# Two attention chunks in plain float32, a pair of heads at a time, and the first halves of batches 0 and 1 ahead of the rest

## The chip, the cores and the metric

One core of one Trainium2 chip runs the whole program. The metric is the device time of one execution in microseconds (us), the median of repeated runs. A profile is one execution, taken by the hardware profiler; its engines are PE (TensorE, with PEld for its weight loads), DVE (VectorE), ACT (ScalarE), POOL (GpSimd) and SP (the queue that issues the DMAs).

## The reference

Windowed attention with a few sink columns, for 4 batches, 8 heads, 768 positions and 64 elements a head, and behind it a two-layer network with a squared ReLU:

```python
keep = is_sink | ((rel >= 0) & (rel < window))       # n_sink = 4, window = 128
scores = np.where(keep, (q @ k.T) / 8, -1e9)         # B, H, S, D = 4, 8, 768, 64
a = np.exp(scores - scores.max(-1)); a = a / (a.sum(-1) + 1e-9)
x = (a @ v)                                          # heads joined: 3072 x 512
out = (s * np.maximum(x @ w_in, 0) ** 2 + b) @ w_out # 512 -> 2048 -> 512
```

Inputs and outputs are float32; `w_in` and `w_out` lie in memory in a form from which the kernel has to make the two float32r parts (a high and a low one) of every weight.

## The kernel before

The 3072 positions are eight **chunks** of 384: two halves of each of the four batches, in the order batch 0 first half, batch 0 second half, batch 1 first half, and so on. For each chunk there is an attention part, which leaves the chunk's `x` as a high and a low float32r part, and a network part of 16 slices `f` of the hidden layer: `l1(f)` (12 products, L521), its squared ReLU (L524 to L529) and `l2(f)` (9 products, L540).

**The first phase** computes chunk 0's attention alone (`first_slots`, L412 on). It works head by head with plain float32 products: `fa` makes the scores of one block of 128 rows (L443; the queries of a head lie on one half of the partitions and the other half is zeroed, L426 and L427), masks them with a running minimum (DVE, L445) and takes exp with its sum (ACT, L449). `fn` forms 1/sum (L457, L458) and scales the rows by it on DVE (L460). `fb` transposes by TensorE (L468) and ACT copies the result out (L472). `fc` multiplies by the values (L480) and splits the result into `x` (L482 on ACT, L483 on DVE). A first half of a batch needs no keys of an earlier block, so its three row blocks see 128, 256 and 384 columns.

**The stages.** Behind that, stage `c` runs the network part of chunk `c` and, between its steps, the attention of chunk `c + 1` (`attn_slots`): the slots of the one are laid between the steps of the other. This attention uses float32r products in two parts. So queries, keys and values are split into a high and a low part (ACT L268, L271, L277; DVE L272; POOL L273, L278), the transposed scores too (ACT L321, DVE L322), sinks are handled apart (POOL L305 and the `psk`, `xsk` lines), and the division comes last (L378 to L384).

**The weights.** In the first phase and in stage 0 the weights are made too (`make_weight`): per slice, two ACT steps (L198, L199), two DVE steps (L200, L201), one POOL step (L203), one ACT step (L208) and a subtraction on DVE, for every fourth slice on POOL (L214). From stage 1 on they are ready.

Instructions go to each engine's queue in an order that a scheduler sets when the program is built; an engine takes its queue in that order. SP issues all DMAs: limits, queries, keys and values of chunk 0, then the scalars `s` and `b`, then weights. A DVE instruction at L682 scales `s`.

```python
for c in range(NC_):
    steps = moe_steps(k.x, store_at(c), wk, before if c == 0 else None, c == NC_ - 1)
    if c + 1 < NC_:
        k, slots = attn_slots(c + 1)
```

## Time and profile before

| | us |
|---|---|
| median of 3 runs (lowest, highest) | 783.11 (782.27, 783.18) |
| the profiled execution | 784.06 |
| its span in the profile | 782.2 |
| PE busy in the span | 736.0 (94%) |
| DVE, ACT, POOL busy | 510.5, 495.0, 263.4 |
| mean granted TensorE clock, share of full | 0.983 |

Busy time is the time in which an engine has an instruction under way. The share of the whole span mixes stages with different limits, so the stages have to be looked at one by one; the stores of each chunk's output mark where a stage ends.

### The profile page before, as it was taken

How to read it: one execution, taken by the hardware profiler on the slowest of the kernel's cores; microseconds unless marked ns; L12 is line 12 of the kernel's file. 1: busy time of each engine (PE TensorE's matmuls, PEld its weight loads, DVE VectorE, ACT ScalarE, POOL GpSimd, SP SyncE). 2: the span in 40 equal slices, each digit the busy share in tenths (PEclk: the TensorE clock that was granted, in tenths of full speed). 3: DMA queues.
4: the chain of work that ended last, by engine and by line, in shares of the span. 5: the costliest groups of instructions: out<-in, count | busy, mean ns of one | idle time of the engine just before them, and what ended most of it. 6: DMA issues, size and time to landing. Idle time of an engine off the chain costs nothing.

```text
span 782.2 us, 12150 instructions
## 1 busy us (share of the span) xinstructions
PE 736.0 (94%) x4036; PEld 656.5 (84%) x4036; DVE 510.5 (65%) x1251; ACT 495.0 (63%) x1231; POOL 263.4 (34%) x411
## 2 busy tenths in 40 slices
PE   6878887599999999999999999999999999999996
PEld 3656675489989999999989999999989999999985
DVE  5888899985676466665676466665676466653321
ACT  4896977766676576656676576656676576643222
POOL 3146567652333234232333234232333234210000
PEclk9998999989999999999999999999999999999999
DMA  7644304212111211112111211112111211001001
GB/s 275 268 148 176 111 14 160 85 34 75 43 44 53 85 47 52 49 43 76 43 43 53 86 47 53 49 43 76 43 43 53 85 47 53 28 1 41 1 1 44
DMA packets 28118, 54.21 MB, mean 69 GB/s; under 512 B 3600, under 2 KB 16528, under 8 KB 26128
## 3 DMA queue, kind: packets, MB, share of 16 engines
q1 hardware_dynamic: 28048, 53.36, 20.8%
q8 instruction: 34, 0.56, 0.3%
q14 instruction: 36, 0.29, 0.1%
HBM read 47.06 MB, written 6.29 MB: 68 GB/s over the span
## 4 chain that ended last, share of the span: by engine, by line
PE 77%; DVE 7%; ACT 6%; POOL 4%; issue 3%; DMA 1%; SPq 1%; POOLq 0%; DVEq 0%; ACTq 0%
PE h L521 31%; PE po L540 30%; PE o L354 5%; PE sc L294 2%; PE sc L293 2%; POOL w L203 2%; PE tp L317 2%; PE tp L316 2%; DVE w L201 1%; ACT w L199 1%; DVE wt L200 1%; PE o L480 1%; DMA sb<-in_s 1%; ACT sm L304 1%; ACT w L208 1%
## 5 line engine op out<-in xcount | busy, mean ns | idle before, releaser
L521 PE MATMUL h<-x,w 128*128 128x384 f32 x1536 | 301.1, 345 | 13.3 <-DVE r L526 7.2
L540 PE MATMUL po<-w,g 128*128 128x512 f32 x1152 | 298.5, 401 | 4.9 <-DVE g L529 3.7
L521 PEld LDWEIGHTS h<-x,w 128*128 128x128 f32 x1536 | 270.8, 191 | 21.4 <-issue 5.4
L540 PEld LDWEIGHTS po<-w,g 128*128 128x128 f32 x1152 | 209.4, 189 | 46.3 <-DVE g L529 5.5
L524 ACT ACTIVATE r<-h 128x384 f32<-128x384 f32 x128 | 62.8, 491 | 110.2 <-PE h L521 103.2
L298 DVE CUSTOM_DVE_ANT_0 sm<-sc,msk 128x272 f32<-128x272 f32 (+1 forms) x168 | 70.2, 418 | 82.4 <-PE sc L294 60.6
L529 DVE SCALAR_TENSOR_TENSOR g<-r,sb,g 128x384 fp32r<-128x384 f32 x128 | 87.2, 681 | 44.7 <-ACT g L528 42.6
L526 DVE SCALAR_TENSOR_TENSOR r<-h,sb,r 128x384 f32<-128x384 f32 x128 | 78.5, 613 | 52.7 <-ACT r L524 52.5
L305 POOL COPY psk<-sm 128x48 f32<-128x48 f32 x168 | 51.8, 309 | 168.4 <-ACT sm L304 167.3
L304 ACT ACTIVATE sm<-sm,negm 128x272 f32<-128x272 f32 (+1 forms) x168 | 85.3, 508 | 22.2 <-DVE negm L298 21.5
L528 ACT ACTIVATE g<-r,sb 128x384 fp32r<-128x384 f32 x128 | 78.8, 615 | 29.3 <-DVE r L526 29.0
L273 POOL TENSOR_TENSOR kl<-kraw,kh 128x544 fp32r<-128x544 f32 (+1 forms) x56 | 71.9, 1283 | 56.4 <-ACT kh L271 54.2
L321 ACT CAST hl<-tp 128x256 fp32r<-128x256 f32 (+1 forms) x168 | 59.1, 353 | 27.2 <-PE tp L317 26.6
L354 PE MATMUL o<-hl,vv 128*128 128x256 f32 (+1 forms) x400 | 71.6, 295 | 1.8 <-DVE hl L322 0.9
L322 DVE TENSOR_TENSOR hl<-tp,hl 128x256 fp32r<-128x256 f32 (+1 forms) x168 | 66.6, 398 | 8.0 <-ACT hl L321 6.1
L278 POOL TENSOR_TENSOR vv<-vraw,vv 128x256 fp32r<-128x256 f32 (+1 forms) x56 | 42.5, 758 | 60.7 <-ACT vv L277 58.7
L354 PEld LDWEIGHTS o<-hl,vv 128*128 128x128 f32 x400 | 55.0, 190 | 4.1 <-issue 1.4
L363 DVE TENSOR_TENSOR xm<-o,y 64x384 f32<-64x384 f32 x56 | 30.9, 552 | 31.5 <-ACT y L362 31.3
L294 PE MATMUL sc<-kl,qs 128*128 128x272 f32 (+1 forms) x168 | 48.7, 290 | 0.4 <-POOL kl L273 0.4
L293 PE MATMUL sc<-kh,qs 128*128 128x272 f32 (+1 forms) x168 | 47.9, 285 | 0.7 <-DVE qs L272 0.4
L272 DVE TENSOR_TENSOR qs<-qraw,qs 64x384 fp32r<-64x384 f32 x56 | 42.4, 758 | 6.2 <-ACT qs L268 4.5
L317 PE MATMUL tp<-identr,sm 128*128 128x128 f32 x168 | 46.0, 274 | 0.0
(113 smaller groups left out, 837.6 us busy)
## 6 DMA issues: line engine op xcount, KB each, us to landing
w<-in_w SPq DMA_DIRECT2D x15, 1024.0 KB, 10.0
kraw<-in_kT SPq DMA_DIRECT2D x32, 272.0 KB, 2.6
out<-ot SPq DMA_DIRECT2D x24, 256.0 KB, 2.0
qraw<-in_qT SPq DMA_DIRECT2D x28, 192.0 KB, 2.3
kraw<-in_kT SPq DMA_DIRECT2D x24, 208.0 KB, 2.4
vraw<-in_v SPq DMA_DIRECT2D x16, 256.0 KB, 2.6
vraw<-in_v SPq DMA_DIRECT2D x12, 192.0 KB, 2.3
vsraw<-in_vsk SPq DMA_DIRECT2D x28, 64.0 KB, 1.8
```

Source lines behind the costliest of these rows:

```text
L273: nc.gpsimd.tensor_tensor(out=hd.kl[:, :kw], in0=hd.k[:, :kw], in1=hd.kh[:, :kw].bitcast(F32), op=ALU.subtract)
L293: nc.tensor.matmul(sc[:, :n], hd.qs[:, qs], hd.kh[:, c0:c0 + n], start=True, stop=False)
L294: nc.tensor.matmul(sc[:, :n], hd.qs[:, qs], hd.kl[:, c0:c0 + n], start=False, stop=True)
L298: nc.vector.tensor_tensor_reduce(out=sm[:, :n], in0=sc[:, :n], in1=m, scale=-0.125, scalar=BIG, op0=ALU.add, op1=ALU.min, accum_out=negm[: ...
L304: nc.scalar.activation(sm[:, :n], sm[:, :n], AF.Exp, bias=negm[:, uu], scale=-1.0, accum_out=pp.zz[:, i, hh:hh + 1])
L322: nc.vector.tensor_tensor(out=lo, in0=tp[:, a:z], in1=hi.bitcast(F32), op=ALU.subtract)
L354: nc.tensor.matmul(hd.o[:, q0:q0 + n * P], hd.vv[:, kb, :], hd.hl[:, t, c0 * P:(c0 + n) * P], start=(hd.n == 0), stop=(i == BLK - 1 and kb ...
L521: nc.tensor.matmul(h[:, :CH], weight[f][:, 0, wi, cc * P:(cc + 1) * P], x[xi][:, cc, :], start=(i == 0), stop=(i == 11))
L526: nc.vector.scalar_tensor_tensor(out=r, in0=h[:, :CH], scalar=sw_ap, in1=r, op0=ALU.mult, op1=ALU.mult)
L528: nc.scalar.activation(gg[:, 0, :], r, AF.Identity, bias=b_ap, scale=1.0)
L529: nc.vector.scalar_tensor_tensor(out=gg[:, 1, :], in0=r, scalar=b_ap, in1=gg[:, 0, :].bitcast(F32), op0=ALU.add, op1=ALU.subtract)
L540: nc.tensor.matmul(po[tb], gg[:, gi, tsl], weight[f][:, 1, wi, :], start=(f == 0 and i == 0), stop=(f == NF - 1 and i == 2))
```

## The change

- The chunks are taken in another order: (0,0), (1,0), (0,1), (1,1), (2,0), (2,1), (3,0), (3,1) as (batch, half). Outputs go to the same places.
- Chunks 0 and 1, both first halves now, are computed by a new class `Plain` in float32 products. Stage 0 so lays plain attention between the network steps, and not the two-part kind.
- `Plain` works on a pair of heads. Its queries and keys lie as loaded: one head on partitions 0 to 63, the other on 64 to 127, and each score product reads one half. The value products write their 64 rows to one half of a bank's partitions, so that a pair shares one bank and one split into `x`.
- The scaling by 1/sum is on GpSimd, six instructions a pair. Of the copies out of the transposes (512 columns each), one in three is on ACT and two on DVE.
- `s` and `b` are loaded behind the first pair's queries and keys. Weight making in the first phase is one step ahead. `xm` has one buffer and not two; the masks stay for the whole program.

```diff
+ORDER = ((0, 0), (1, 0), (0, 1), (1, 1), (2, 0), (2, 1), (3, 0), (3, 1))
-E0, LB0, LC0 = 8, 4, 6
+E0 = 8
+FN, FB, FC = (4, 2), (6, 6), (9, 10)
-    m_all = first.tile([P, 6 * P], MDT, tag="m", name="m_all")
+    m_all = const.tile([P, 6 * P], MDT, tag="m", name="m_all")
-        k.c, k.b, k.half = c, c // 2, c % 2
+        k.c, (k.b, k.half) = c, ORDER[c]
-                pp.x = wk.tile([P, CH], F32, tag="xm", name="xm")
+                pp.x = wk.tile([P, CH], F32, tag="xm", name="xm", bufs=1)
-    def first_slots():
...
+    class Plain:
...
+            self.groups = ((0, 1, 2),) if c == 0 else ((0, 1), (2,))
...
+        def scores(self, pr, group):
...
+            for i in self.groups[group]:
+                for hh in range(2):
+                    hs = slice(hh * D, (hh + 1) * D)
+                    j = (i // 2, hh)
+                    if j not in banks:
+                        banks[j] = ps("sc")
+                    c0, n = (0, P, 0)[i], (i + 1) * P
+                    nc.tensor.matmul(banks[j][:, c0:c0 + n], pp.q[hs, i * P:(i + 1) * P], pp.k[hs, :n], start=True, stop=True)
...
+                    nc.vector.tensor_tensor_reduce(out=sm, in0=banks[(i // 2, hh)][:, c0:c0 + n], in1=m_full[i], scale=-0.125, scalar=BIG,
+                                                   op0=ALU.add, op1=ALU.min, accum_out=negm[:, uu])
+                    nc.scalar.activation(sm, sm, AF.Exp, bias=negm[:, uu], scale=-1.0, accum_out=pp.z[:, 0, i, hh:hh + 1])
+        def norm(self, pr):
+            pp = self.pairs[pr]
+            nc.vector.tensor_scalar(out=pp.z[:, 1], in0=pp.z[:, 0], scalar1=1e-9, scalar2=None, op0=ALU.add)
+            nc.vector.reciprocal(out=pp.z[:, 0], in_=pp.z[:, 1])
+            for i in range(BLK):
+                c0, n = (0, P, 0)[i], (i + 1) * P
+                for hh in range(2):
+                    sm = pp.sm[2 * (i // 2) + hh][:, c0:c0 + n]
+                    nc.gpsimd.tensor_scalar(out=sm, in0=sm, scalar1=pp.z[:, 0, i, hh:hh + 1], scalar2=None, op0=ALU.mult)
+        def turned(self, pr, part):
...
+            pos = (((0, 0), (2, 2)), ((1, 0), (1, 1)), ((2, 0), (2, 1)))[part]
+            for hh in range(2):
+                for j, (i, kb) in enumerate(pos):
+                    c0 = (0, P, 0)[i] + kb * P
+                    nc.tensor.transpose(tp[:, (2 * hh + j) * P:(2 * hh + j + 1) * P], pp.sm[2 * (i // 2) + hh][:, c0:c0 + P], ident)
...
+            cp = nc.scalar.copy if part == 0 else nc.vector.tensor_copy
+            cp(out, tp.rearrange("p (h k c) -> p h k c", h=2, c=P))
+        def values(self, pr):
...
+            for kb in range(BLK):
+                for hh in range(2):
+                    a = (0, 3, 5)[kb]
+                    hs = slice(hh * D, (hh + 1) * D)
+                    nc.tensor.matmul(o[hs, kb * P:CH], pp.v[:, kb, hh], pp.t[:, hh, a:a + BLK - kb].rearrange("p k c -> p (k c)"),
+                                     start=(kb == 0), stop=(kb == BLK - 1))
+            nc.scalar.copy(self.x[0][:, pr, :], o[:, :CH])
+            nc.vector.tensor_tensor(out=self.x[1][:, pr, :], in0=o[:, :CH], in1=self.x[0][:, pr, :].bitcast(F32), op=ALU.subtract)
...
-    k, slots = first_slots()
+    k, slots = plain_slots(0)
+    k.load_first(slice(0, 1))
+    nc.sync.dma_start(sb[:, 0:1], s.partition_broadcast(P))
+    nc.sync.dma_start(sb[:, 1:2], b.partition_broadcast(P))
+    constants()
+    k.load_first(slice(1, NCC))
+    k.load_values()
...
-        if i >= 22 and i % 2 == 0:
-            weights(NEARLY - 1, (i - 20) // 2)
+        if i >= 20 and i % 2 == 0:
+            weights(NEARLY - 1, (i - 18) // 2)
...
-            k, slots = attn_slots(c + 1)
+            k, slots = plain_slots(1) if c == 0 else attn_slots(c + 1)
```

The first place where rows move is SP's queue at the program's start. Before (`q_102`, `q_103`, `k_106`, `v_107` are chunk 0's queries of even and odd heads, keys and values, the first load of each the first pair's; `sb` holds `s` and `b`; `w_` are raw weights):

```order
L431 DMA q_102<-in_qT 64x384
L433 DMA k_106<-in_k 128x384
L431 DMA q_103<-in_qT 64x384
L434 DMA v_107<-in_v 128x384
L431 DMA q_102<-in_qT 64x3x384
L433 DMA k_106<-in_k 128x1152
L431 DMA q_103<-in_qT 64x3x384
L434 DMA v_107<-in_v 128x3x384
L493 DMA sb<-in_s 128x1
```

With the change:

```order
L431 DMA q_102<-in_qT 128x384
L432 DMA k_103<-in_k 128x384
L721 DMA sb<-in_s 128x1
L722 DMA sb<-in_b 128x1
L431 DMA q_102<-in_qT 128x3x384
L432 DMA k_103<-in_k 128x1152
```

The load of `s` moved from ninth to third place among these.

The second place is ACT's queue at the end of the first phase, up to the last pair's `x`. Before (`w4` to `w7` are tiles of raw weights, `x0_0` is the high part of chunk 0's `x`, `vs`, `qs`, `kh`, `vv` are chunk 1's split operands):

```order
L259 CAST vs_565<-vsraw_563 128x128
L268 CAST qs_568<-qraw_556 64x384
L271 CAST kh_570<-kraw_561 128x544
L482 CAST x0_0_104<-o0_498 64x384
L472 COPY tt0_490<-tp0_511 128x3x128
L277 CAST vv_575<-vraw_558 128x4x64
L198 ACTIVATE w4_263<-w4_263 128x1024
L199 ACTIVATE w4_263<-w4_263 128x1024
L482 CAST x0_0_104<-o0_518 64x384
```

With the change (`tf` is the copied transpose):

```order
L201 ACTIVATE w4_246<-w4_246 128x1024
L520 CAST x0_0_105<-o_403 128x384
L200 ACTIVATE w5_397<-w5_397 128x1024
L201 ACTIVATE w5_397<-w5_397 128x1024
L210 CAST w2_512<-w3_244 128x2x512
L200 ACTIVATE w6_399<-w6_399 128x1024
L509 COPY tf_414<-tp_415 128x2x2x128
L201 ACTIVATE w6_399<-w6_399 128x1024
L200 ACTIVATE w7_401<-w7_401 128x1024
L201 ACTIVATE w7_401<-w7_401 128x1024
L520 CAST x0_0_105<-o_442 128x384
```

The raw weights up to `w7` are now begun ahead of the last `x`, where before `w4` was the last. The whole queue up to that `x` holds 17 weight instructions with the change (seven each of L200 and L201, three of L210) and held 10 before (four of L198, four of L199, two of L208); the four casts for chunk 1 are gone.

The third place is POOL's queue in stage 0, with the change (`w6_399` and the like are raw weights, `smf` the exp'd scores of pair 0 of chunk 1, `zf` its 1/sum):

```order
L205 TENSOR_TENSOR w6_399<-w6_399 128x1024
L205 TENSOR_TENSOR w7_401<-w7_401 128x1024
L494 TENSOR_SCALAR smf_496<-smf_496,zf_489 128x128
L494 TENSOR_SCALAR smf_499<-smf_499,zf_489 128x128
L494 TENSOR_SCALAR smf_496<-smf_496,zf_489 128x256
L494 TENSOR_SCALAR smf_499<-smf_499,zf_489 128x256
L494 TENSOR_SCALAR smf_574<-smf_574,zf_489 128x384
L494 TENSOR_SCALAR smf_577<-smf_577,zf_489 128x384
L205 TENSOR_TENSOR w8_549<-w8_549 128x1024
```

The scalings of a pair stand as a block between weight steps, where before copies into `psk` and subtractions for keys, values and `x` stood.

## Rows read from the trace of the kernel before

**Rows 1.** The busy time of each engine by stage. The columns are: the stretch in us, its length, then busy us and instruction count of PE, PEld, DVE, ACT, POOL, the granted TensorE clock as a share of full, the DMA share and GB/s. The stretches are stage 0, stage 1 (beside the attention of a first half), stage 2 (beside that of a second half) and the last stage (no attention).

```profile
49.50:179.50 130.00, 104.86 (x517) 86.06 (x516) 117.02 (x196) 97.94 (x200) 82.37 (x74) 0.93 0.32 111
179.50:266.00 86.50, 86.01 (x494) 79.21 (x493) 55.39 (x148) 55.95 (x152) 28.12 (x52) 1.00 0.18 55
266.00:355.40 89.40, 89.08 (x518) 82.29 (x517) 57.64 (x148) 58.37 (x152) 29.38 (x52) 1.00 0.18 55
707.20:782.20 75.00, 68.47 (x342) 61.21 (x340) 19.94 (x33) 21.00 (x38) 1.01 (x1) 0.98 0.06 23
```

**Rows 2.** The timeline of the SP queue: the stores of a chunk's output, three at the end of each stage (start in us, length).

```profile
179.51 3.09 SPq L638 DMA_DIRECT2D out<-ot  x3
...
265.99 3.08 SPq L638 DMA_DIRECT2D out<-ot  x3
```

**Rows 3.** DVE in stage 0, by line and shape: output and inputs, count | busy us, mean ns | idle time before. These are lines of the two-part attention.

```profile
L272 DVE TENSOR_TENSOR qs<-qraw,qs 64x384 fp32r<-64x384 f32 x9 | 12.9, 1431 | 0.3
L298 DVE CUSTOM_DVE_ANT_0 sm<-sc,msk 128x272 f32<-128x272 f32 x24 | 10.4, 432 | 2.6 <-PE sc L294 2.3
...
L322 DVE TENSOR_TENSOR hl<-tp,hl 128x256 fp32r<-128x256 f32 x24 | 9.7, 414 | 0.1
...
L363 DVE TENSOR_TENSOR xm<-o,y 64x384 f32<-64x384 f32 x8 | 4.4, 549 | 0.1
...
L381 DVE TENSOR_TENSOR xm<-os,xm 128x384 f32<-128x384 f32 x4 | 2.2, 553 | 0.9 <-PE os L378 0.9
L382 DVE TENSOR_TENSOR xm<-zb,xm 128x384 f32<-128x384 f32 x4 | 2.2, 552 | 0.2
L370 DVE TENSOR_TENSOR xsk<-ts,xsk 32x384 fp32r<-32x384 f32 x4 | 2.2, 550 | 0.1
...
L298 DVE DVE_READ_ACCUMULATOR2_ANT negm<- 128x1 f32 x24 | 1.9, 80 | 0.0
```

**Rows 4.** DVE in the first phase, by line and shape, same columns.

```profile
L483 DVE TENSOR_TENSOR x<-o,x 64x384 fp32r<-64x384 f32 x8 | 4.4, 551 | 1.2 <-ACT x L482 0.9
L445 DVE CUSTOM_DVE_ANT_0 sm<-sc,m_all 128x384 f32<-128x384 f32 x8 | 4.4, 548 | 0.3 <-PE sc L443 0.2
L460 DVE TENSOR_SCALAR sm<-sm,z 128x128 f32<-128x128 f32 x8 | 4.2, 531 | 0.1
...
L445 DVE CUSTOM_DVE_ANT_0 sm<-sc,m_all 128x256 f32<-128x256 f32 x8 | 3.4, 420 | 1.3 <-PE sc L443 1.2
L460 DVE TENSOR_SCALAR sm<-sm,z 128x384 f32<-128x384 f32 x8 | 3.3, 411 | 0.0
L460 DVE TENSOR_SCALAR sm<-sm,z 128x256 f32<-128x256 f32 x8 | 2.8, 345 | 0.0
...
L445 DVE CUSTOM_DVE_ANT_0 sm<-sc,m_all 128x128 f32<-128x128 f32 x8 | 2.3, 284 | 1.7 <-PE sc L443 1.7
...
L445 DVE DVE_READ_ACCUMULATOR2_ANT negm<- 128x1 f32 x24 | 2.0, 81 | 0.0
L458 DVE RECIPROCAL z<-z 128x3 f32<-128x3 f32 x8 | 1.4, 174 | 0.2
...
L457 DVE TENSOR_SCALAR z<-z 128x3 f32<-128x3 f32 x8 | 1.3, 162 | 0.0
```

**Rows 5.** The timeline of TensorE in the first phase (start, length, instructions merged): six transposes, the value products of one head (six instructions, two for each of 384, 256 and 128 columns), and what starts behind them.

```profile
21.23 0.82 PE L468 MATMUL tp<-identr,sm 128*128 128x128 f32 x6
21.89 0.82 PE L443 MATMUL sc<-k,q 128*128 128x128 f32 x4
22.55 1.46 PE L480 MATMUL o<-tt,v 128*128 128x384 f32 x6
23.84 0.60 PE L468 MATMUL tp<-identr,sm 128*128 128x128 f32 x4
```

**Rows 6.** TensorE in the first phase, by line and shape: the longest form of the score products.

```profile
L443 PE MATMUL sc<-k,q 128*128 128x384 f32 x16 | 7.0, 520 | 0.0
```

**Rows 7.** The timeline of DVE: the instruction that scales `s`, with the idle time before it and what ended it.

```profile
13.34 0.15 DVE L682 TENSOR_SCALAR sb<-sb 128x1 f32<-128x1 f32 x1 [3.54 <-DMA sb<-in_s]
```

**Rows 8.** The timeline of ACT at the end of the first phase: a weight step, and the last high part of chunk 0's `x`.

```profile
49.36 1.13 ACT L199 ACTIVATE w<-w 128x1024 f32<-128x1024 f32 x1
50.51 0.48 ACT L482 CAST x<-o 64x384 fp32r<-64x384 f32 x1
```

**Rows 9.** ACT in the first phase, by line and shape.

```profile
L482 ACT CAST x<-o 64x384 fp32r<-64x384 f32 x8 | 3.8, 476 | 0.7 <-PE o L480 0.4
L472 ACT COPY tt<-tp 128x384 f32<-128x384 f32 x8 | 3.8, 475 | 0.1
...
L472 ACT COPY tt<-tp 128x256 f32<-128x256 f32 x8 | 2.9, 366 | 0.2 <-PE tp L468 0.2
...
L472 ACT COPY tt<-tp 128x128 f32<-128x128 f32 x8 | 2.1, 266 | 1.4 <-PE tp L468 1.3
```

**Rows 10.** POOL in stage 0, by line and shape: a subtraction with two inputs.

```profile
L384 POOL TENSOR_TENSOR x<-xm,x 128x384 fp32r<-128x384 f32 x3 | 4.3, 1421 | 2.6 <-ACT x L383 2.6
```

**Rows 11.** POOL in the first phase: a fill, which writes and reads nothing.

```profile
L140 POOL MEMSET psk<- 128x384 f32 x2 | 0.8, 418 | 0.1
```

**Rows 12.** The timeline of all engines in stage 2: the last reader of one pair's `xm`, and the first writer of the next pair's.

```profile
341.97 1.02 POOL L384 TENSOR_TENSOR x<-xm,x 128x384 fp32r<-128x384 f32 x1
...
344.62 0.54 DVE L363 TENSOR_TENSOR xm<-o,y 64x384 f32<-64x384 f32 x1
```

More of the change, by code (lines that the diff above doesn't have):

```diff
@@ new lines, in norm @@
+        def norm(self, pr):
+            pp = self.pairs[pr]
+            nc.vector.tensor_scalar(out=pp.z[:, 1], in0=pp.z[:, 0], scalar1=1e-9, scalar2=None, op0=ALU.add)
+            nc.vector.reciprocal(out=pp.z[:, 0], in_=pp.z[:, 1])
+            for i in range(BLK):
+                c0, n = (0, P, 0)[i], (i + 1) * P
+                for hh in range(2):
+                    sm = pp.sm[2 * (i // 2) + hh][:, c0:c0 + n]
+                    nc.gpsimd.tensor_scalar(out=sm, in0=sm, scalar1=pp.z[:, 0, i, hh:hh + 1], scalar2=None, op0=ALU.mult)
@@ new lines, in turned @@
+        def turned(self, pr, part):
+            pp = self.pairs[pr]
+            if part == 0:
+                pp.t = (wk if self.c else first).tile([P, 2, 2 * BLK, P], F32, tag="hl" if self.c else "tt0", name="tf", bufs=2)
+            tp = (ps if self.c else po_bank)("tp")
+            pos = (((0, 0), (2, 2)), ((1, 0), (1, 1)), ((2, 0), (2, 1)))[part]
[3 more added lines that the diff above has]
+                    nc.tensor.transpose(tp[:, (2 * hh + j) * P:(2 * hh + j + 1) * P], pp.sm[2 * (i // 2) + hh][:, c0:c0 + P], ident)
+            out = pp.t[:, :, part:part + (6 if part == 0 else 3):(5 if part == 0 else 2)]
+            cp = nc.scalar.copy if part == 0 else nc.vector.tensor_copy
+            cp(out, tp.rearrange("p (h k c) -> p h k c", h=2, c=P))
@@ new lines, in values @@
+        def values(self, pr):
+            pp = self.pairs.pop(pr)
+            o = ps("o")
+            for kb in range(BLK):
+                for hh in range(2):
[5 more added lines that the diff above has]
+            nc.vector.tensor_tensor(out=self.x[1][:, pr, :], in0=o[:, :CH], in1=self.x[0][:, pr, :].bitcast(F32), op=ALU.subtract)
@@ new lines, in po_bank, with plain_slots, at @@
+    def po_bank(name):
+        return psO.tile([P, 512], F32, tag="po", name=name)
+    def plain_slots(c):
+        k = Plain(c)
+        k.turn = 0
+        todo = {}
+        def at(t, fn, *a):
+            todo.setdefault(max(t, 0), []).append((fn, a))
+        first_one = c == 0
+        for pr in range(H // 2):
+            t = 6 * pr
+            at(t - (0 if first_one else 6), k.load, pr)
+            for g in range(len(k.groups)):
+                at(t + 2 * g, k.scores, pr, g)
+            for part in range(3):
+                at(t + FB[first_one] + part, k.turned, pr, part)
+            at(t + FN[first_one], k.norm, pr)
+            at(t + FC[first_one], k.values, pr)
@@ L488, in slot @@
         def slot(t):
             def f():
-                if t == 0:
-                    load()
-                    constants()
-                    nc.sync.dma_start(sb[:, 0:1], s.partition_broadcast(P))
-                    nc.sync.dma_start(sb[:, 1:2], b.partition_broadcast(P))
-                if t < n:
-                    fa(*units[t])
-                if t % BLK == BLK - 1 and t < n:
-                    for i in range(BLK):
-                        fn(t // BLK, i)
-                if 0 <= t - LB0 < n:
-                    fb(*units[t - LB0])
@@ L503, in f @@
-                if 0 <= t - LC0 < n and (t - LC0) % BLK == BLK - 1:
-                    fc((t - LC0) // BLK)
+                for fn, a in todo.get(t, ()):
+                    fn(*a)
             return f
-        return k, [slot(t) for t in range(n + LC0)]
+        return k, [slot(t) for t in range(max(todo) + 1)]
     def moe_steps(x, store, wk, before=None, last=False):
@@ L636, in f @@
         def f(tb, ot):
-            r0 = c * CH + tb * P
+            r0 = (2 * ORDER[c][0] + ORDER[c][1]) * CH + tb * P
             nc.sync.dma_start(out[r0:r0 + P, :], ot)
```

105 lines of the change are left out of this document (45 added, 60 removed).

## The prediction

> **What bounds the kernel now.** I read the busy times by stage first, since the share of the whole span hides that there are two kinds of stage. From stage 1 on TensorE is busy for 86.0 of 86.5 us or 89.1 of 89.4 us, at full clock, and DVE and ACT for only some 56 to 58 us [rows 1]: there only TensorE's work counts. Stage 0 is different: 130.0 us, with DVE busy for 117.0 (0.90), TensorE for 104.9 at a mean clock of 0.93, and POOL for 82.4 [rows 1]. Weight making and the two-part attention both sit on DVE there, and TensorE waits. The stage boundaries are the stores of a chunk's output [rows 2]. The last stage, which has no attention, takes 68.5 us of TensorE; so the attention beside stage 1 costs 17.5 us of it and the one beside stage 2 20.6 us. The first phase, up to 49.5 us, is a chain over all engines: nobody is full, and one stall stands in the DVE queue, 3.54 us in front of the scaling of `s`, because the load of `s` lands late [rows 7].
>
> The sums are made against the profiled execution, 784.06 us, which is 0.95 us above the median of the runs, 783.11.
>
> **Stages 1 to 7.** Stage 1 now runs beside the attention of (0,1), a second half, where it ran beside (1,0), a first half. The five stages behind it keep their kinds. So one stage of 86.5 us becomes one of 89.4 us: **+2.9 us**, certain as long as TensorE sets these stages. `xm` with one buffer adds a wait in the DVE queue: the next pair's first write (L363) behind POOL's last read (L384). At the closest pass that I found in stage 2, the read ends at 342.99 us and the write begins at 344.62 us [rows 12], so 1.6 us are left and I cost it at nothing. Without that cover, scores and splits queued behind L363 on DVE would wait, and TensorE for them.
>
> **Stage 0, DVE.** Out go the two-part lines: the `qs` splits (8 of the 9, 11.5 us), masks 10.4 and their accumulator reads 1.9, `hl` 9.7, and the four lines of `xm` and `xsk` 11.0; together 44.5 us [rows 3]. In come, for one plain chunk: masks 4.4 + 3.4 + 2.3 and accumulator reads 2.0, so 12.1 us; half of the 1/sum lines, 1.4 us, since a pair shares them; the splits of `x`, four of 384 columns on 128 partitions, half of 4.4 us, 2.2 [rows 4]. The copies of 512 columns on DVE have no row. Their bounds: 0.55 us, the two-input read of 384 columns, from below, and 0.73 us, the same stretched to 512 columns, from above; the masks grow by 264 ns from 128 to 384 columns, which gives 548 + 132 = 680 ns [rows 4]. I take 0.68 us, 8 of them, 5.4 us. In all 21.1 us come in, and DVE falls from 117.0 to **93.6 us**.
>
> **Stage 0, TensorE.** The network part is 68.5 us [rows 1]. A plain chunk costs per head: six value instructions, started 1.29 us ahead of what follows them, and six transposes, 0.66 us [rows 5]. The scores have the same columns as the values, so 1.29 us again. That is 3.24 us a head, 25.9 us for eight, and **94.4 us** in all. It is 5.3 us more than the two-part chunk took, and it counts only because DVE no longer hides it. No instruction of before uses half the array, so its price is bounded: from below by two heads running side by side, which halves scores and values (10.3 us less), from above by nothing overlapping at all. A score product of 384 columns takes 520 ns alone [rows 6], where the stream passes 384 columns in 1.29 x 384/1536 = 0.32 us; 0.20 us more for each of the 96 instructions is 19.2 us. I take the stream as it runs before, between the two.
>
> **Stage 0, POOL and ACT.** POOL loses the `psk` copies and the splits of keys and values and gets 24 scalings of 768 columns a head. A fill of 384 columns takes 418 ns [rows 11], a two-input subtraction of 384 columns in stage 0 takes 1421 ns [rows 10]; so a head costs between 0.84 and 2.84 us and a chunk between 6.7 and 22.7 us. I take 9.6 us, nearer the fill, because there is one input. That is far from filling POOL, and DVE is relieved of stretching beside it. ACT was at 97.9 of 130 us [rows 1], loses more than it gets, and does not bind. On SP a pair of the plain chunk has three loads where the two-part kind had five; they have one buffer each, so the load of the next pair's values waits for this pair's value products, and the raw weights of later slices stand behind it in the queue. I cost that at nothing: a pair has a quarter of the stage, some 25 us, and these weights are used later still; if they came late, ACT's weight steps would wait and the network steps behind them.
>
> **Stage 0, sum.** Two engines at 94 us and two with air. A full stage under one bound reaches 0.99 [rows 1], DVE now reaches 0.90; with two engines nearly level I take 0.92, near the latter, so 94.4 / 0.92 = 102.6 us. **-27.4 us**.
>
> **First phase.** Its end is the last high part of `x` on ACT, which starts at 50.51 us and ends at 51.0 us [rows 8]. Up to there ACT's queue loses the copies of the transposes, 8.8 us, for four of 512 columns (475 + 128 x 0.82 = 580 ns, 2.3 us), so -6.5 us; half of the `x` casts, -1.9 us [rows 9]; and chunk 1's four casts, which I estimate from the length of the `x` cast of 476 ns at -1.9 us. It gains seven weight instructions of 1.13 us, +7.9 us [rows 8]. The load of `s` is issued ahead of the long loads, so the stall of 3.5 us goes; the next thing late there is the queries and keys of the other pairs, which are issued at about the same time as before. DVE loses the scalings, 10.3 us [rows 4], but a pair's scalings now stand on POOL between exp and transposes. That gives -6.5 - 1.9 - 1.9 + 7.9 - 3.5 = **-5.9 us**. Both ends are kept: nothing, if the chain over POOL costs what the stall gave, and -11 us, if the weight steps fill gaps. The seven steps are not done again in stage 0, where ACT had air.
>
> **Sum.** 784.06 + 2.9 - 27.4 - 5.9 = 753.7 us for the profiled execution, and 0.95 less, **752.7 us**, for the median.
>
> **The rivals.**
> - *A break at each change between full and half array.* A break in TensorE's stream costs 0.20 us [rows 5, 6]. Three visits to half-array products a pair make 12 visits and 24 changes, 4.8 us; TensorE then needs 99.2 us, stage 0 takes 99.2 / 0.92 = 107.8, and the median is 757.9 us. The Trainium skill, TensorEngine Tiling (Array Packing), Key Properties, speaks for this one: changing the tiling mode drains TensorE. No run here shows it so far.
> - *Two heads side by side.* The score products of the two heads alternate and go to different banks, and the value products alternate between halves of the columns. If they overlap, TensorE needs 84.1 us in stage 0 and DVE binds alone with 93.6; at 0.95 the stage is 98.5 us, and the median 748.6 us. Against it: DVE stays where it was, so little is won. The Trainium skill, same page and list, says that tiles in different parts of the array work in parallel; no run here shows that either.
> - *No overlap at all.* 19.2 us more on TensorE, 113.6 us at 0.95 are 119.6 us: 769.7 us.
> - *Something else held stage 0.* The weight chain crosses ACT, DVE, POOL, ACT and DVE for each slice. If its order, and not DVE's fullness, sets the pace, the stage only falls to some 115 us: 765.1 us. For it: ACT waits are spread over the stage; against it: DVE was at 0.90.
> - *Slower.* No overlap and the clock falls: short half-array products with breaks let the granted clock go to its lower level of 1.2 GHz. The mean clock is 0.93 in stage 0 now, so the gate does act there [rows 1]. The case before leaves 783.1 - 769.7 = 13.4 us to today's result, and each microsecond of work at the lower level takes one more, so it decides from some 13 us of work at that level on. A third of 113.6 us there makes 113.6 x 1.333 / 0.95 = 159.4 us, and the median 809.5 us. Against it: the network products stay in between and keep TensorE busy.
>
> **Chances.** My forecast, with its own range of 747 to 759 us (first phase between 0 and -11), 0.45; breaks at the changes 0.16; side by side 0.18; no overlap 0.06; weight chain 0.07; slower 0.06; and 0.02 that the terms cancel. The range of 739 to 770 us takes in the first five: its lower end is side by side with the first phase at -11 us and less stretching on DVE, its upper end the no-overlap case. Faster than before by more than 0.2%, which is about what a measurement of this kernel can tell, 0.92; within it 0.02; slower 0.06.
>
> **What would show it.** In the profile of the changed kernel: stage 0 at some 100 us with TensorE and DVE both over 0.9; stage 1 at 89.4 us; the stores of chunk 0 at about 146 us; no wait for `s` in DVE's queue; POOL's scalings of 256 columns at some 0.4 us; the plain products in stage 0 at 1.3 us a head or, side by side, at half. Wrong would be: stage 0 still over 115 us, TensorE waiting there for POOL's scalings, a clock below 0.9 in it, or gaps on TensorE from stage 1 on behind a late `xm`.

## The result, and the profile after

The kernel before took 783.17 us (median of 9 runs), the changed one 787.35 us (785.65 to 789.81, 9 runs). The ratio is 1.0054, 95% interval 1.0039 to 1.0069: **slower by 0.5%**, where I had forecast 752.7 us and had named 739 to 770 as the range. (One run of experiment e12 below took 1165 us, at a mean granted clock of 0.56, and is left out of its median.)

The busy times by stage of the changed kernel, in the columns of [rows 1]; the boundaries are the first network product (L565, at 62.20 us) and the stores:

```profile
0.00:62.20 62.20, 38.49 (x158) 20.11 (x158) 30.15 (x105) 34.88 (x74) 33.90 (x49) 0.68 0.43 166
62.20:179.20 117.00, 98.50 (x481) 78.07 (x480) 82.59 (x146) 69.29 (x135) 70.99 (x47) 0.88 0.29 105
179.20:268.70 89.50, 89.16 (x517) 82.17 (x516) 57.80 (x148) 58.23 (x153) 29.97 (x53) 1.00 0.23 67
709.90:784.80 74.90, 68.45 (x342) 61.20 (x340) 19.94 (x33) 20.98 (x38) 1.02 (x1) 0.97 0.06 23
```

Read from the bottom: the last stage is what it was, and stage 1 grew by 3.0 us, as forecast. Stage 0 fell, but from 130.0 to 117.0 us only, and no engine is full in it: DVE has 82.6 us of 117 (0.71), TensorE 98.5 (0.84) at a granted clock of 0.88. The first phase grew from 49.5 to 62.2 us, and in it every engine is busy for at most 0.62. A stage with no full engine is a chain of waits. The first stores of chunk 0's output, in the form of [rows 2], stand where they stood before (179.51 us), though I had forecast some 146; the second line is chunk 1's:

```profile
179.24 0.87 SPq L682 DMA_DIRECT2D out<-ot  x2
...
268.72 3.04 SPq L682 DMA_DIRECT2D out<-ot  x3
```

The waits of the first 185 us (who waited for whom: us in total, times, longest; L506 are the transposes, L509 the copies out of them) name the chain:

```profile
ACT tf L509 <- PE tp L506: 30.2, 7, 7.1
...
PE tp L506 <- POOL sm L494: 16.0, 15, 2.6
...
PE tp L506 <- POOL smf L494: 14.8, 6, 5.2
DVE tf L509 <- PE tp L506: 13.7, 6, 4.6
```

TensorE stands still 30.8 us in front of its transposes until POOL's scalings come (`sm` is chunk 0, `smf` chunk 1), and ACT and DVE stand behind these transposes in turn. Not all of the 16.0 us of the first phase are new, since before the change TensorE waited there for DVE's scalings:

```profile
PE tp L468 <- DVE sm L460: 8.1, 4, 4.5
```

What one scaling takes on POOL, by shape, for the first phase and then stage 0 (columns as in [rows 4]):

```profile
L494 POOL TENSOR_SCALAR sm<-sm,zf 128x384 f32<-128x384 f32 x8 | 9.8, 1241 | 0.0
L494 POOL TENSOR_SCALAR sm<-sm,zf 128x256 f32<-128x256 f32 x8 | 8.2, 1042 | 0.0
...
L494 POOL TENSOR_SCALAR sm<-sm,zf 128x128 f32<-128x128 f32 x8 | 4.7, 602 | 7.1 <-DVE zf L489 5.1 <-ACT w L200 2.0
...
L494 POOL TENSOR_SCALAR smf<-smf,zf 128x128 f32<-128x128 f32 x8 | 11.4, 1440 | 10.3 <-ACT w L201 6.0 <-DVE zf L489 4.3
L494 POOL TENSOR_SCALAR smf<-smf,zf 128x384 f32<-128x384 f32 x8 | 9.8, 1238 | 0.0
L494 POOL TENSOR_SCALAR smf<-smf,zf 128x256 f32<-128x256 f32 x8 | 8.9, 1126 | 0.0
```

A chunk costs 9.8 + 8.2 + 4.7 = 22.7 us in the first phase and 30.1 us in stage 0, where I had 9.6. One scaling of 384 columns (1241 ns) is three times the 411 ns that DVE needed [rows 4], and longer than the two-input subtraction of the same shape at its fastest, 1.02 us [rows 12]. The 7.4 us that stage 0 has more are nearly all in the form of 128 columns (1440 ns against 602). POOL's first scalings run there beside DVE's weight steps, so the last section may bear on them; no run takes this apart. What that does to TensorE is seen in its timeline in stage 0 (in brackets the idle time before an instruction and what ended it; L565 and L584 are the network products, L466 the scores):

```profile
79.48 2.03 PE L565 MATMUL h<-x,w 128*128 128x384 f32 x10 [0.59 <-DVE w L216]
85.27 0.48 PE L506 MATMUL tp<-identr,smf 128*128 128x128 f32 x1 [3.76 <-POOL smf L494]
89.98 0.69 PE L506 MATMUL tp<-identr,smf 128*128 128x128 f32 x2 [4.24 <-POOL smf L494]
91.20 0.47 PE L506 MATMUL tp<-identr,smf 128*128 128x128 f32 x1 [0.53 <-POOL smf L494]
91.60 1.65 PE L466 MATMUL sc<-kf,qf 64*128 64x128 f32 x8
93.19 3.35 PE L584 MATMUL po<-w,g 128*128 128x512 f32 x7
```

and POOL's in the same stretch:

```profile
76.14 2.20 POOL L205 TENSOR_TENSOR w<-w 128x1024 int32<-128x1024 int32 x1 [1.16 <-DVE w L203]
81.25 1.89 POOL L205 TENSOR_TENSOR w<-w 128x1024 int32<-128x1024 int32 x1 [2.90 <-DVE w L203]
83.12 8.03 POOL L494 TENSOR_SCALAR smf<-smf,zf 128x128 f32<-128x128 f32 x6
91.12 1.89 POOL L205 TENSOR_TENSOR w<-w 128x1024 int32<-128x1024 int32 x1
```

The six scalings of a pair take 8.03 us in a row. They start only when POOL is through with a weight step that itself waited 2.90 us for DVE. TensorE takes its queue in order: the transposes stand ahead of the network products of L584, so these wait too. And the next weight step on POOL starts at 91.12 us, behind the block. One slow block so holds two chains, and the granted clock falls behind such gaps: TensorE is busy for 2.0 us between 80 and 90 us and for 4.2 between 110 and 120, and the ten microseconds behind each have a clock of 0.61 and 0.75. Ten-microsecond windows, columns as above:

```profile
20.00:30.00 10.00, 6.48 (x30) 3.62 (x30) 3.42 (x5) 5.50 (x7) 8.24 (x7) 0.50 1.00 414
...
40.00:50.00 10.00, 6.86 (x25) 3.52 (x24) 4.87 (x9) 4.59 (x14) 4.11 (x4) 0.50 0.00 0
...
80.00:90.00 10.00, 2.01 (x11) 1.39 (x9) 7.05 (x9) 4.53 (x7) 8.75 (x7) 0.70 0.23 97
90.00:100.00 10.00, 9.47 (x37) 7.29 (x38) 5.22 (x13) 6.25 (x14) 5.23 (x3) 0.61 0.00 0
...
110.00:120.00 10.00, 4.23 (x21) 3.29 (x20) 6.92 (x8) 3.08 (x4) 10.00 (x7) 0.91 0.30 105
120.00:130.00 10.00, 9.47 (x44) 7.76 (x45) 6.57 (x13) 6.56 (x16) 7.24 (x4) 0.75 0.11 28
```

At a clock of 0.50, the lower level of 1.2 GHz, TensorE's work takes about twice as long. The value products of a pair, first at the lower level and then at the full one:

```profile
47.23 2.83 PE L518 MATMUL o<-tf,v 128*64 128x384 f32 x12 [0.88 <-DVE tf L509]
...
105.76 1.52 PE L518 MATMUL o<-tf,vf 128*64 128x384 f32 x12
```

### The profile page after: what moved, and what is told of

The parts are those of the page before. It is cut to its first block, busy times and chain, and to the rows that moved or that the text cites. A ratio compares the mean times of both kernels' runs of the same rounds, so it can differ in the third digit from the quotient of the medians.

```text
span 784.8 us, 11909 instructions
## 1 busy us (share of the span) xinstructions
PE 733.9 (94%) x4024; PEld 647.0 (82%) x4024; DVE 473.2 (60%) x1174; ACT 467.7 (60%) x1147; POOL 274.1 (35%) x406
## 4 chain that ended last, share of the span: by engine, by line
PE 80%; POOL 5%; DVE 5%; ACT 4%; issue 2%; POOLq 0%; ACTq 0%; DVEq 0%
PE h L565 32%; PE po L584 31%; PE o L356 5%; POOL smf L494 3%; PE sc L296 2%; PE sc L295 2%; PE tp L319 2%; PE tp L318 2%; POOL sm L494 2%; PE o L518 1%; DVE w L203 1%; PE tp L506 1%; PE ts L369 1%; PE sc L466 1%; PE os L380 1%
## 5 line engine op out<-in xcount | busy, mean ns | idle before, releaser
L565 PE MATMUL h<-x,w 128*128 128x384 f32 x1536 | 298.9, 344 | 3.7 <-ACT tf L509 3.1
L584 PE MATMUL po<-w,g 128*128 128x512 f32 x1152 | 296.2, 402 | 0.0
L565 PEld LDWEIGHTS h<-x,w 128*128 128x128 f32 x1536 | 271.1, 190 | 9.8 <-ACT tf L509 3.3
L584 PEld LDWEIGHTS po<-w,g 128*128 128x128 f32 x1152 | 210.8, 190 | 44.4 <-issue 1.3
L573 DVE SCALAR_TENSOR_TENSOR g<-r,sb,g 128x384 fp32r<-128x384 f32 x128 | 80.9, 632 | 54.0 <-ACT g L572 52.6
L300 DVE CUSTOM_DVE_ANT_0 sm<-sc,msk 128x272 f32<-128x272 f32 (+1 forms) x144 | 60.9, 423 | 74.9 <-PE sc L296 63.7
L307 POOL COPY psk<-sm 128x48 f32<-128x48 f32 x144 | 35.9, 249 | 162.5 <-ACT sm L306 161.7
L306 ACT ACTIVATE sm<-sm,negm 128x272 f32<-128x272 f32 (+1 forms) x144 | 73.7, 512 | 24.4 <-DVE negm L300 22.6
L275 POOL TENSOR_TENSOR kl<-kraw,kh 128x544 fp32r<-128x544 f32 (+1 forms) x48 | 60.8, 1266 | 62.1 <-ACT kh L273 57.2
L323 ACT CAST hl<-tp 128x256 fp32r<-128x256 f32 (+1 forms) x144 | 51.3, 356 | 27.9 <-PE tp L319 27.4
L324 DVE TENSOR_TENSOR hl<-tp,hl 128x256 fp32r<-128x256 f32 (+1 forms) x144 | 58.0, 403 | 9.5 <-ACT hl L323 7.8
L356 PE MATMUL o<-hl,vv 128*128 128x256 f32 (+1 forms) x352 | 61.8, 294 | 0.0
L280 POOL TENSOR_TENSOR vv<-vraw,vv 128x256 fp32r<-128x256 f32 (+1 forms) x48 | 34.6, 721 | 53.4 <-ACT vv L279 51.0
L205 POOL TENSOR_TENSOR w<-w 128x1024 int32<-128x1024 int32 (+1 forms) x17 | 31.8, 1872 | 30.6 <-DVE w L203 15.1
L295 PE MATMUL sc<-kh,qs 128*128 128x272 f32 (+1 forms) x144 | 40.4, 281 | 0.0
```

Source lines behind the costliest of these rows:

```text
L275: nc.gpsimd.tensor_tensor(out=hd.kl[:, :kw], in0=hd.k[:, :kw], in1=hd.kh[:, :kw].bitcast(F32), op=ALU.subtract)
L300: nc.vector.tensor_tensor_reduce(out=sm[:, :n], in0=sc[:, :n], in1=m, scale=-0.125, scalar=BIG, op0=ALU.add, op1=ALU.min, accum_out=negm[: ...
L306: nc.scalar.activation(sm[:, :n], sm[:, :n], AF.Exp, bias=negm[:, uu], scale=-1.0, accum_out=pp.zz[:, i, hh:hh + 1])
L324: nc.vector.tensor_tensor(out=lo, in0=tp[:, a:z], in1=hi.bitcast(F32), op=ALU.subtract)
L356: nc.tensor.matmul(hd.o[:, q0:q0 + n * P], hd.vv[:, kb, :], hd.hl[:, t, c0 * P:(c0 + n) * P], start=(hd.n == 0), stop=(i == BLK - 1 and kb ...
L565: nc.tensor.matmul(h[:, :CH], weight[f][:, 0, wi, cc * P:(cc + 1) * P], x[xi][:, cc, :], start=(i == 0), stop=(i == 11))
```

## The experiments

My theory after the result, called A: POOL's slow scalings stand in the chain, and with a faster engine in their place the change is worth most of what I forecast. B: POOL is one delay among several; the clock, the order or the plain products would hold the time anyway. Twelve kernels were run. Their phases, from one profile each (start of the first network product; from there to the first store of chunk 0's output), and their medians and ratios to the kernel before, beside which each was run (the median of the first row is the one beside the change):

| | first phase | stage 0 | median | ratio (95%) |
|---|---|---|---|---|
| before | 49.5 | 130.0 | 783.17 | 1 |
| the change | 62.2 | 117.0 | 787.35 | 1.0054 (1.0039, 1.0069) |
| e1 scaling on VectorE | 46.8 | 110.1 | 764.34 | 0.9766 (0.9739, 0.9793) |
| e2 chunk 1 alone on VectorE | 62.5 | 106.6 | 776.08 | 0.9913 (0.9896, 0.9929) |
| e3 twice the POOL work | 68.7 | 126.7 | 803.73 | 1.0272 (1.0254, 1.0289) |
| e4 scaling on ScalarE | 47.7 | 117.1 | 768.52 | 0.9805 (0.9772, 0.9837) |
| e5 POOL, later transposes | 54.7 | 117.3 | 781.45 | 0.9968 (0.9951, 0.9984) |
| e6 POOL, clock kept up | 61.2 | 118.7 | 788.67 | 1.0066 (1.0048, 1.0083) |
| e7 e1, heads one after the other | 52.6 | 109.3 | 768.80 | 0.9821 (0.9787, 0.9855) |
| e8 e1, chunk 1 in two parts | 51.2 | 115.1 | 773.31 | 0.9873 (0.9843, 0.9904) |
| e9 e1, late `s` | 44.0 | 110.2 | 761.64 | 0.9722 (0.9697, 0.9747) |
| e10 e1, weights later | 45.2 | 113.9 | 767.49 | 0.9800 (0.9778, 0.9823) |
| e11 before, new order of chunks | 50.6 | 116.6 | 773.97 | 0.9876 (0.9854, 0.9897) |
| e12 e1, subtractions to POOL | 46.8 | 112.5 | 768.20 | 0.9824 (0.9791, 0.9856) |

Two cautions on the phases. The runs of one kernel differ by up to some 5 us (e1: 762.07 to 766.74) and each has one profile, so a difference of 2 or 3 us between two phases shows little by itself. And the first network product does not need the last `x`. The mark of the prediction, the end of the last high part of `x` on ACT, comes 0.5 to 1.5 us later, in e1 and e9 2.5 us; in what follows it is called the last `x`, and where the two marks tell different things, both are given.

**e1: the scaling on VectorE.** One word, and the rest of the change as it is:

```diff
-                    nc.gpsimd.tensor_scalar(out=sm, in0=sm, scalar1=pp.z[:, 0, i, hh:hh + 1], ...)
+                    nc.vector.tensor_scalar(out=sm, in0=sm, scalar1=pp.z[:, 0, i, hh:hh + 1], ...)
```

> Scaling by 1/sum on VectorE in both plain chunks, nothing else. Theory A (the scalings on GpSimd, 5.4 us a pair in the first phase and up to 9.3 us in stage 0, stand in front of TensorE's transposes and so of everything behind them): 1.8 us a pair on VectorE; first phase from 62 to some 47 us, stage 0 from 117 to some 100 us, 755 us in all (748 to 765), the granted clock above 0.9 in both. Theory B (thin half-array products and the lower clock that goes with them are the cause, wherever the scaling is): the clock stays at 0.7 in the first phase and the time within 5 us of the changed kernel, 780 to 790 us.

764.34 us: the sign of the change turns by moving six instructions a pair, 23.0 us by the medians. That is in A's range, near its upper end, and far from B's. Two marks of A were missed: stage 0 is at 110.1 us and not at some 100, and the clock of the first phase is 0.82 and not above 0.9. The windows of e1, first phase and stage 0:

```profile
0.00:46.80 46.80, 32.16 (x159) 18.37 (x159) 35.70 (x126) 34.27 (x73) 12.37 (x25) 0.82 0.57 221
46.80:156.90 110.10, 96.15 (x480) 75.32 (x480) 99.18 (x174) 69.78 (x136) 42.51 (x23) 0.95 0.30 111
```

DVE is busy for 16.6 us more in stage 0 than in the changed kernel, and the stage is 6.9 us shorter. DVE's share is 0.90 again, as before [rows 1].

**e2: chunk 1's scaling on VectorE, chunk 0's on POOL.**

```diff
+                    (nc.vector if self.c else nc.gpsimd).tensor_scalar(...)
```

> Scaling on VectorE in chunk 1 only; chunk 0 keeps GpSimd. A: the first phase stays at 62 us, stage 0 gets to some 100 us, 770 us in all (762 to 775). B: 780 to 790 us.

776.08 us, 1.1 us above A's range, but it splits the loss. The first phase stays at 62.5 us, so chunk 0's scaling on POOL costs 15.7 us there against e1 (13.8 by the last `x`). Stage 0 falls from 117.0 to 106.6, so chunk 1's costs 10.4 us here; between the changed kernel and e1 the same stage falls by 6.9 only. Stage 0 of e2:

```profile
62.50:169.10 106.60, 95.86 (x480) 75.58 (x479) 90.75 (x170) 68.37 (x135) 43.98 (x23) 0.94 0.32 115
```

**e3: twice the POOL work.** A scaling by 1.0 ahead of each.

```diff
+                    nc.gpsimd.tensor_scalar(out=sm, in0=sm, scalar1=1.0, scalar2=None, op0=ALU.mult)
                     nc.gpsimd.tensor_scalar(out=sm, in0=sm, scalar1=pp.z[:, 0, i, hh:hh + 1], ...)
```

> Each scaling on GpSimd preceded by a second one by 1.0 of the same size; the output is unchanged. A: some 5.4 us more for each of four pairs in the first phase and 5.4 to 9 us in stage 0, and nearly all of it in the time: 820 to 840 us. B: GpSimd was at 0.54 and 0.61 of the two stretches and has room; under 10 us more, 787 to 797 us.

803.73 us, between the two ranges. POOL's busy time grew by 22.1 us in the first phase and 26.0 us in stage 0, and the time by 16.4 us, a third of that. The test was not clean: a scaling by 1.0 does not need 1/sum, so it may run beside the exps of later rows.

**e4: the scaling on ScalarE.**

```diff
+                    nc.scalar.activation(sm, sm, AF.Identity, scale=pp.z[:, 0, i, hh:hh + 1])
```

> Scaling on ScalarE in both plain chunks. A: some 2.6 us a pair on ScalarE, whose queue then also holds exp and weight steps; first phase some 50 us, stage 0 some 103 us, 760 us (752 to 772), a little above VectorE's. B: 780 to 790 us.

768.52 us, inside the range. The first phase is as good as e1's (47.7). Stage 0 is not (117.1): ACT has 90.5 us there, where e1 has 69.8, and DVE is hardly relieved (96.5 against 99.2). The test moved more than the scaling: the scheduler put 6 weight instructions ahead of the last `x` in ACT's queue, where e1 has 17, so the rest of them is in stage 0 with the scalings of chunk 1 (10.0 us). And the profiled run was the longest of the four, 3.8 us above the median.

**e5: the transposes later in the queue.** The scaling stays on POOL; its users come later. (`i < 29` keeps the number of weight steps that the program issues in the first phase.)

```diff
-FN, FB, FC = (4, 2), (6, 6), (9, 10)
+FN, FB, FC = (2, 2), (7, 9), (10, 13)
-        if i >= 20 and i % 2 == 0:
+        if 20 <= i < 29 and i % 2 == 0:
```

> Scaling stays on GpSimd; only the slots move: in chunk 1 the scalings are issued two slots earlier and the transposes one slot later, in chunk 0 the transposes three slots later, behind the next pair's scores. If the loss is TensorE standing in its queue before a transpose whose scaling isn't done, TensorE's waits for GpSimd fall by half or more and the time to 770 to 780 us. If GpSimd's work as such sets the pace (5.4 us a pair and more, whatever the order), 784 to 792 us.

781.45 us, between the ranges, nearer to the queue theory. The first phase gave back 7.5 of its 12.7 us. In stage 0 TensorE's wait for `smf` fell from 14.8 to 4.9 us, and the stage stayed at 117.3. A wait stands elsewhere now, in ACT's weight step behind POOL's, for which the changed kernel waited 8.8 us:

```profile
ACT w L210 <- POOL w L205: 25.4, 10, 6.4
...
PE tp L506 <- POOL sm L494: 12.0, 11, 4.0
```

So TensorE standing in its queue explains at most these 7.5 us of the first phase, and less wait of TensorE did not shorten stage 0. More can't be read from it, since the scheduler moved weight steps as well: 11 weight instructions of ACT stand ahead of the last `x`, where the changed kernel has 17, and the other six fall into stage 0.

**e6: the clock kept up.** 16 products on unused data ahead of each pair's transposes in the first phase; their results go nowhere.

```diff
+            if part == 0 and not self.c:
+                wt = po_bank("wt0")
+                for _ in range(16):
+                    nc.tensor.matmul(wt, warm[:, :P], warm, start=True, stop=True)
```

> The changed kernel with 16 dummy products a pair (128x512, bfloat16, no result used) queued on TensorE ahead of chunk 0's transposes, where it waits for GpSimd. The granted clock was 0.68 in the first phase; TensorE is busy for 38.5 of its 62.2 us. If the lower clock is a part of the loss of its own, the first phase shortens by some 5 us in spite of the dummies (780 to 784 us). If only the wait for GpSimd counts, the first phase stays or grows (786 to 795 us).

788.67 us, no gain. The granted clock of the first phase rose from 0.68 to 0.86 and its length went from 62.2 to 61.2 us. The 64 added products took 16.1 us of TensorE, and the rest of its busy time there fell from 38.5 to 29.9 us. What faster products gave may have gone into the added ones, so the run does not show what the low clock costs by itself. It shows that no time is won in this way.

**e7: two heads one after the other.** On e1, the loops over blocks and heads change places in scores and values, so that neighbours no longer lie on different halves.

```diff
-            for kb in range(BLK):
-                for hh in range(2):
+            for hh in range(2):
+                for kb in range(BLK):
```

> The kernel with the scaling on VectorE (764.3 us), with all products of one head of a pair first and those of the other after it, in scores and values, in place of alternating heads. If two half-array products of different halves run side by side, a pair's twelve value instructions go from 1.45 to some 2.6 us, likewise the scores, some 9 us more TensorE work in stage 0, and 767 to 775 us. If they don't, nothing changes: 762 to 766 us.

768.80 us against 764.34, in the range of the side-by-side theory. The value products of a pair at full clock, e1 first, then e7:

```profile
153.67 1.52 PE L518 MATMUL o<-tf,vf 128*64 128x384 f32 x12
```

```profile
141.92 2.21 PE L518 MATMUL o<-tf,vf 128*64 128x384 f32 x12
```

The scores gain less: the twelve score products of the first pair go from 1.57 to 1.90 us at full clock, and the two groups of a pair in stage 0 stay at 0.93 and 0.92 us. Most of the 4.5 us came from the first phase, which is 5.8 us longer (3.9 by the last `x`), and little from stage 0, which is 0.8 shorter (1.2 longer). The value products of the four pairs of the first phase, in part at the lower clock, take 2.83, 1.52, 2.83 and 1.52 us in e1 and 4.14, 3.15, 3.85 and 2.21 in e7: 4.7 us together. TensorE's own work counts in the first phase, which is a chain; of the 0.7 us and more that each pair's values cost in stage 0 little or nothing shows.

**e8: two-part attention for chunk 1.** On e1.

```diff
-            k, slots = plain_slots(1) if c == 0 else attn_slots(c + 1)
+            k, slots = attn_slots(c + 1)
```

> The kernel with the scaling on VectorE, with the two-part attention for chunk 1 (batch 1, first half) as before, so only chunk 0 is plain. If the plain chunk 1 is what shortens stage 0, that stage goes from 110 to some 125 us and the time to 776 to 784 us. If the gain over before came from the first phase alone, 762 to 768 us.

773.31 us, in neither range: the plain chunk 1 is worth 9.0 us, 5.0 of it in stage 0 and 4.4 in the first phase (7.0 and 2.5 by the last `x`). Stage 0 is at 115.1 even without plain attention, far from 130.0. That led to e11.

**e9, e10: two terms of the first phase.** Both on e1: `s` and `b` loaded behind all queries, keys and values; weight making one step later.

```diff
+    k.load_values()
+    nc.sync.dma_start(sb[:, 0:1], s.partition_broadcast(P))
+    nc.sync.dma_start(sb[:, 1:2], b.partition_broadcast(P))
```

> The kernel with the scaling on VectorE (764.3 us), and the loads of `s` and `b` issued behind all queries, keys and values of chunk 0, as before the change. If the early load was worth what the sum gave it, the wait for `s` is back in VectorE's queue and the time is 766.5 to 768.5 us (+3.5). If another wait had taken the place of that stall: 763 to 765.5 us.

761.64 us, below both ranges: not slower than e1, and if anything faster (the intervals of the two ratios overlap). DVE does not wait for `s` in either, since the instruction that scales it now stands later in the queue. TensorE's wait for the second pair's keys tells where the early load went. e1 first, then e9:

```profile
11.09 1.58 PE L466 MATMUL sc<-k,q 64*128 64x128 f32 x12 [2.90 <-DMA k<-in_k]
```

```profile
9.44 1.58 PE L466 MATMUL sc<-k,q 64*128 64x128 f32 x12 [0.92 <-DMA k<-in_k]
```

```diff
-        if i >= 20 and i % 2 == 0:
-            weights(NEARLY - 1, (i - 18) // 2)
+        if i >= 22 and i % 2 == 0:
+            weights(NEARLY - 1, (i - 20) // 2)
```

> The kernel with the scaling on VectorE (764.3 us), and weight making in the first phase one step later, as before the change. The sum charged the first phase +7.9 us for the added weight steps and gave stage 0 nothing for them. If that is right, the first phase ends 5 to 8 us earlier and stage 0 is at most 2 us longer: 757 to 761 us. If the steps only move, or if they fill gaps on ScalarE: 763 to 770 us, with stage 0 longer by as much as the first phase is shorter, or more.

767.49 us, in the second range (the intervals of this ratio and e1's overlap): the first phase is 1.6 us shorter and stage 0 3.8 us longer. But the edit did less than its lines say. The scheduler still puts 16 weight instructions ahead of the last `x` in ACT's queue, where e1 has 17 and the kernel before 10. The end of ACT's first phase, e1 first, then e10:

```profile
47.77 1.15 ACT L210 CAST w<-w 128x1024 fp32r<-128x1024 f32 x1 [1.29 <-DVE w L216]
48.82 0.48 ACT L520 CAST x<-o 128x384 fp32r<-128x384 f32 x1
```

```profile
45.19 1.15 ACT L201 ACTIVATE w<-w 128x1024 f32<-128x1024 f32 x1
46.23 0.46 ACT L520 CAST x<-o 128x384 fp32r<-128x384 f32 x1
```

The one step that left, with the wait in front of it, is 2.4 of the 2.6 us by which the last `x` ends earlier. So e10 prices one of the seven added weight instructions, and six stay untested; why stage 0 is 3.8 us longer it does not show either.

**e11: the new order of chunks alone, in the kernel before.**

```diff
-        k.c, k.b, k.half = c, c // 2, c % 2
+        k.c, (k.b, k.half) = c, ORDER[c]
```

> The kernel before with the new order of chunks alone: all attention as before, but the two-part attention of stage 0 is that of batch 1's first half. The kernel with a two-part chunk 1, the new order and the scaling on VectorE had a stage 0 of 115.1 us where the kernel before had 130.0. If a first half in stage 0 is what made it shorter (fewer instructions on VectorE, which binds there), stage 0 falls by 8 to 15 us, stage 1 grows by 2.9, and the time is 772 to 778 us. If it was the weight step made earlier, stage 0 stays over 125 us and the time is 782 to 787 us.

773.97 us, as the first theory had it. One part of the change, with no plain chunk in stage 0 and no POOL scaling, is 9.2 us faster than the kernel before. Its stages 0 and 1:

```profile
50.61:167.18 116.57, 96.28 (x493) 81.14 (x492) 109.62 (x196) 95.72 (x200) 85.38 (x74) 0.96 0.35 119
167.18:256.57 89.39, 89.07 (x518) 82.28 (x517) 57.71 (x148) 58.57 (x152) 30.23 (x52) 1.00 0.20 59
```

A first half beside stage 0 takes 7.4 us off DVE, and the stage falls by 13.4; stage 1 pays 2.9.

**e12: more weight subtractions on POOL.** On e1.

```diff
-                e = nc.gpsimd if f % 4 == 3 else nc.vector
+                e = nc.gpsimd if f % 2 == 1 else nc.vector
```

> The kernel with the scaling on VectorE (764.3 us), where the weight subtraction of every second slice is on GpSimd, and not of every fourth: four subtractions of 1.2 us leave VectorE, four of 2.6 us come to GpSimd. If VectorE's fullness sets stage 0 (99 of 110 us), the time falls by 3 to 5 us, to 759 to 761.5 us. If GpSimd's longer time in the weight chain costs as much, or more: 764 to 769 us.

768.20 us, in the second range and slower than e1 by 3.9 (the two intervals just touch). DVE's busy time in stage 0 did not fall by some 5 us but from 99.2 to 98.5. The last section shows a reason that fits.

## Why the prediction was wrong

**The step that failed** is the one on POOL: "I take 9.6 us, nearer the fill, because there is one input. That is far from filling POOL", and in the first phase "a pair's scalings now stand on POOL between exp and transposes", which I left out of the sum. POOL's time for it was 22.7 us in the first phase and 30.1 in stage 0, at and over my upper bound of 22.7 [rows 10]. The fill [rows 11] reads nothing and says little of an instruction that reads its data. The greater error was the kind of question: I asked whether POOL would be full. It was not, with 71.0 of 117 us. But six scalings in a row are 5.4 to 9.3 us between an exp and a transpose, and behind that transpose, in stage 0, TensorE's network products wait. Such a delay has to be laid against the path and not against a share. With the scaling on DVE (e1) or ACT (e4) the same change is 23.0 or 18.8 us faster. e1 still lies 11.6 us above the forecast, so POOL is about two thirds of the miss, and the rest is in the two sums below. The slower case that I named, no overlap and a falling clock, had the right sign and the wrong mechanism: the values of two heads overlap (e7). The clock did fall, to 0.68 and 0.88, but with POOL's waits gone it is 0.82 and 0.95 with the same products (e1); what it costs by itself stays open (e6).

**Stage 1, +2.9 us:** right, 3.0 measured. `xm` with one buffer costs nothing that shows: in stage 1 TensorE is busy for 89.16 of 89.5 us.

**Stage 0, -27.4 us:** measured -13.0; with the scaling on DVE -19.9. The sum let TensorE and DVE set the stage, at 0.92. In e1 DVE has 0.90 of it, as before; in the changed kernel it has 0.71. That DVE's work alone sets the stage is not shown even for e1: in e2 it has 0.85 of a shorter stage, and in e12 its busy time hardly fell when work was taken off it. DVE's own sum was off as well, 82.6 us measured for 93.6. It left the four lines that make 1/sum for the two-part kind in (4.9 us), and line L573 of the network took 11.2 us in the changed kernel, where it had 17.6 before, for the same 16 instructions; in e1 it has 17.5 again. The split of the gain I did not see: of the 19.9 us some two thirds belong to the order of chunks (e11, 13.4 us), which the sum booked under the two-part lines of a second half, and 5.0 to the plain chunk (e8 to e1; 7.0 by the last `x`).

**First phase, -5.9 us:** measured +12.7 (+11.8 by the last `x`, which is the sum's own mark). Without the POOL term the sum came close, -2.7 us in e1 and -5.5 in e9 (-1.7 and -4.5), but that does not bear it out. It adds up what ACT's queue gains and loses, as if ACT set the phase, and ACT is idle for 14.2 of 49.5 us before, for 27.3 of 62.2 with the change and for 12.5 of 46.8 in e1. The early load of `s` was to give 3.5 us; the wait passed to the keys, and undoing it made the phase 2.8 us shorter (e9). I had named the next late thing and then put its cost at nothing. What the seven weight instructions cost, 7.9 us in the sum, no run shows: all 17 are still there in e1 and e9, and e10 takes away one.

**TensorE.** A pair's value products take 1.52 us, where I took 2 x 1.29 [rows 5] and gave side by side 0.18. It was right as a mechanism for the values, at 1.45 times the speed of e7's order. By the rule of the Trainium skill that I had set beside it, TensorEngine Tiling (Array Packing), Key Properties, tiles in different parts of the array work in parallel; the trace agrees. It was of little worth in stage 0, as its own line said. The break at a change of tiling is smaller than I priced it, at least for the values. The chain of waits of the changed kernel (start, us, what):

```profile
158.41 2.11 PE h L565 x12
160.53 1.45 PE o L518 x12
161.97 2.29 PE po L584 x9
164.26 2.11 PE h L565 x12
166.38 2.09 PE po L584 x9
```

The network step behind a pair's values takes 2.29 us, an undisturbed one 2.09; the step ahead of them has its usual 2.11. That is 0.20 us a visit where I had 0.40.

**Open.** How much of e4's stage 0 of 117.1 us, with no engine over 0.88 of it, is the weight steps that moved into it was not taken apart. Of the 3.5 us by which e2's stage 0 is shorter than e1's, 1.9 are the mark (e1's last `x` comes late behind the first network product); the rest, with DVE busy for 90.75 us and not 99.18, is open.

## What to carry to other kernels

Before an operation goes to an idle engine, lay its whole block (count x duration there) between the instruction that feeds it and the one that waits, and look up what stands behind the waiting one in its in-order queue; the engine's busy share does not answer this. Where there is no row for the operation on that engine, take the dearer neighbour: the two-input row was near, and the fill was not. Even a copy would have misled, since POOL's copies of 128 bfloat16 columns took 292 to 294 ns in the kernel before, and its scalings of 128 float32 columns 602. Count in the queue what an edit has moved before pricing a term by it: a scheduler put the same weight steps elsewhere in e4 and e5, and left them where they were in e10. And run the parts of a change alone: here an order of chunks, one line of numbers, carried as much (9.2 us, e11) as the plain attention of chunk 1 (9.0, e8 to e1), and a bundle that measures as slightly slower held some 20 us of gain.
